# Attention and MLP on one core: seven early attention slots take the interleaved form of the later ones

## The chip, the cores and the metric

The kernel runs on one core of a Trainium2 chip. Its engines work side by side, each through its own queue in order: TensorE (PE: matmuls, with PEld for its weight loads), VectorE (DVE), ScalarE (ACT), GpSimd (POOL), and SyncE (SP), which issues DMAs. Matmuls write into banks of PSUM, an accumulator memory of eight banks here, which DVE and ACT read. An engine that has to wait for another one waits on a semaphore, and everything behind the waiting instruction in its queue waits with it. The metric is the time of one execution on the device, in microseconds (us).

## What is computed

Attention with normalised queries and keys, and after it an MLP whose activation is h - tanh(h):

```python
batch, n_heads, seq, head_dim = (8, 12, 448, 64)
q_n, k_n = (rmsnorm(q, g_q), rmsnorm(k, g_k))
scores = scale * np.matmul(q_n, k_n.transpose(0, 1, 3, 2))
attn = np.exp(scores - np.max(scores, axis=-1, keepdims=True))
attn = attn / (np.sum(attn, axis=-1, keepdims=True) + 1e-09)
attn_out = np.matmul(attn, v)
x = attn_out.transpose(0, 2, 1, 3).reshape(B * S, H * D)   # 3584 x 768
h = x @ w_in                                                # 768 x 2048
g = h - np.tanh(h)
out = g @ w_out                                             # 2048 x 768
```

All matmuls are in float32. In the profile each of them shows as two records, so "x16" in a row of PE stands for 8 matmuls.

## The kernel before

**Slots.** Attention is worked off in 48 slots, six for each of the eight batches; a slot `s` is one pair of heads of one batch. `NP` is 6, so slots 0 to 5 are the first batch, 6 to 11 the second, and so on. The MLP of batch b runs while the attention of batch b + 1 is computed. The MLP is one generator, `stream`; `run(ns)` takes matmuls from it until they are worth `ns` of PE's time. So the order of all instructions on each engine is written out by hand: a slot issues some attention work, then a stretch of the MLP ("a gap"), then attention work again. There is no scheduler after that.

**Three kinds of slot.** `first_slot` (slots -3 to 5) runs before any MLP; it also begins to round the weights (L71 and L72 on ACT, L78 to L82 on DVE, L90 on POOL, in this order for each piece). `early_slot` (6 to 11) runs beside the first batch's MLP, in which the rest of the weights is still rounded, combined (L339) and kept. `slot` (12 to 47) runs beside the others. `FOLDED` is 13: from there on a slot sums its exponentials in another way (`fold` and what follows), so that no sums are taken on PE. Four gaps make up a slot. In slots 6 to 8 a gap is 14 matmuls of 224 columns (`L791`, the first layer of the MLP, 28 records); in slots 9 to 11 it is 8 matmuls of 448 columns (`L969`, the second layer of the first batch, 16 records).

**What a slot computes.** For its two heads, with 448 keys in four chunks (three of 128, numbered 0 to 2, and a last one `KF` of 64 keys for each of the two halves of the queries):
- `scores(s + 1, c)` (L528): keys times queries of the next slot, in tiles of 64 rows and 32 columns of the array, into two banks, one for each head (`L542`); then an exponential on ACT for each bank (`L548`). Its result goes to `p` (chunks 0 and 1), `p_full` (chunk 2) and `p_last`.
- `totals(s)` (L654): the sums over the keys, as matmuls with ones (`L669`), into one bank, and a reciprocal on DVE (`L674`). Up to slot 9 there are 16 matmuls in it, later 4, because from slot 10 on DVE has added up the exponentials before (`add`, `add_last`).
- `last_values` and `values(s)` (L588, L639): values times probabilities. `values` uses tiles of 128 rows and 32 columns (`L646`): all 128 keys of a chunk at once, each bank of `av` taking one half of the queries (224 columns).
- `divide(s)` (L717): four multiplications on DVE (`L730`) take `av` times the reciprocal into `xT`, the MLP's input; for the last three pairs of heads of a batch, POOL forms sums of it (`tt`, L744 to L747).
- `turn(s + 2)` (L438): keys and queries of the slot after the next are transposed on PE (`L443`, `L447`) into two banks, and copied by ACT.

**The visit.** From slot 13 on, `visit` (L620) does values and the next slot's scores together. `half_values` (L601) takes the values in tiles of 64 rows and 32 columns (`L608`): each of the two banks of `av` gets half of the keys and all 448 queries. Four such tiles and four of the scores fit the array side by side, and `wave` issues them alternately. `divide` then adds the two banks: ACT copies one into `xT` (L722), DVE adds the other (L723), and DVE multiplies (L727).

**Banks.** Three banks (`mm`) are for the MLP. Five (`sc`) are for attention, and `sc_bank()` hands them out in turn; an engine that writes a bank waits until the reader of its former content is done. Up to slot 11 all five rotate, and `av` is two of them. Before slot 12, L1143 sets two aside as `av_banks`, so that three rotate.

**Order in an early slot.** `totals(s)`, scores of chunks 0 and 1 of the next slot, the load of v for s + 2, a gap, `turn(s + 2)` and squares, a gap, scores of chunk `KF`, `last_values`, `values`, `divide`, scores of chunk 2, and then two gaps in four halves with additions and norms between them (`add`, `add_last`, `norm`, `norm_q`; the last of these is eight scalings on ACT, `L430`, in slots 6 to 11).

Of the kernel before, what the change touches and what calls it, by code (L numbers as in the profile page):

```python
# [144 lines left out]
def bounded_path(tc, ctx, q, k, v, moe_w_in, moe_w_out, out, g_col, ident, ones, half_ones, neg_half, early):  # L145
# [379 lines left out]
    def sc_bank():  # L525
        return bank_of("sc")

    def scores(s, c, apart=False):  # L528

        rr, kT, qT = turned[s]  # L530
        n = S if c < KF else HS
        name, bufs = ("p", 2) if c < 2 else ("p_full", 1) if c < KF else ("p_last", 2)
        if c == 1:
            p = probs[s, 1] = probs[s, 0]
        else:
            p = probs[s, c] = pp.tile([P, 2, 2 if c < 2 else 1, n], F32, name=name, bufs=bufs)
        tiles = [sc_bank() for _ in range(2)]

        def score(h, i):
            at, first = (i * BL, 0) if c < KF else (i * BL % KR, i * BL // KR * n)  # L540
            r = slice(h * D, (h + 1) * D)
            nc.tensor.matmul(  # L542
                tiles[h][i * BL : (i + 1) * BL, :n], lhsT=kT[r, c * P + at : c * P + at + BL],
                rhs=qT[r, first : first + n], start=True, stop=True,
            )

        def exp(h):
            nc.scalar.activation(  # L548
                p[:, h, c if c < 2 else 0, :], tiles[h][:, :n], AF.Exp,
                scale=1.0 if rr is None else rr[:, 0, 2 * c + h : 2 * c + h + 1],  # L550
            )

        if apart:
            return [(lambda i, h=h: score(h, i), lambda h=h: exp(h)) for h in range(2)]
        for i in range(P // BL):
            for h in range(2):
                score(h, i)
        for h in range(2):
            exp(h)
# [28 lines left out]
    def last_values(s, av):  # L588

        v_nat, p = loaded["v", s], probs[s, KF]  # L590
        for n in range(2):
            keys, at = slice(n * KR, (n + 1) * KR), n * HS if s >= FOLDED else 0
            for m in range(2):
                for h in range(2):
                    r = (2 * m + h) * BL
                    nc.tensor.matmul(  # L596
                        av[n][r : r + BL, at : at + HS], lhsT=v_nat[keys, h, KF, m * BL : (m + 1) * BL],
                        rhs=p[keys, h, 0], start=(s < FOLDED), stop=False, skip_group_check=(s >= FOLDED),
                    )

    def half_values(s, c, av, first):  # L601
# [37 lines left out]
    def values(s, av, chunks=(2, 0, 1)):  # L639
        v_nat, p = loaded["v", s], full(s)  # L640
        for c in chunks:
            for n in range(2):
                for m in range(2):
                    for h in range(2):
                        r = (2 * m + h) * BL
                        nc.tensor.matmul(  # L646
                            av[n][r : r + BL, :HS], lhsT=v_nat[:, h, c, m * BL : (m + 1) * BL],
                            rhs=p[c][:, h, n * HS : (n + 1) * HS], start=False, stop=(c == 1),
                        )
        if 1 in chunks:  # L650
            del loaded["v", s]
        return av
# [21 lines left out]
        nc.vector.reciprocal(rs, dn[:, :HS])  # L674


    FOLDED = 2 * NP + 1

    def fold(s):

# [36 lines left out]
    def divide(s, av):  # L717
        b, hp = steps[s]
        rs = whole.pop(s)
        x = xT[b, hp] = xp.tile([P, S], F32, name="xT")  # L720
        if s >= FOLDED:
            nc.scalar.copy(out=x, in_=av[0][:, :S])  # L722
            nc.vector.tensor_tensor(out=x, in0=x, in1=av[1][:, :S], op=ALU.add)  # L723
        for m in range(2):
            rows = slice(m * D, (m + 1) * D)
            if s >= FOLDED:
                nc.vector.tensor_tensor(out=x[rows], in0=x[rows], in1=rs, op=ALU.mult)  # L727
                continue
            for n in range(2):
                nc.vector.tensor_tensor(  # L730
                    out=x[rows, n * HS : (n + 1) * HS], in0=av[n][rows, :HS], in1=rs[n * D : (n + 1) * D],
                    op=ALU.mult,
                )
        for c in range(NCH):
            del probs[s, c]
        if hp < HC:
            return
        c = hp - HC
        if c == 0:
            tt[b] = tp.tile([P, 3, HC, HS], F32, name="tt", bufs=1)  # L740
        eng = nc.vector if b == 0 and c == HC - 1 else nc.gpsimd
        x11, x12, x21, x22 = (xT[b, r][:, n : n + HS] for r in (c, hp) for n in (0, HS))
        t1, t2, t4 = (tt[b][:, i, c] for i in range(3))
        eng.tensor_tensor(out=t1, in0=x12, in1=x11, op=ALU.subtract)  # L744
        eng.tensor_tensor(out=t2, in0=x22, in1=t1, op=ALU.subtract)  # L745
        eng.tensor_tensor(out=x12, in0=x22, in1=x12, op=ALU.subtract)
        eng.tensor_tensor(out=t4, in0=x21, in1=t2, op=ALU.subtract)  # L747
# [264 lines left out]
    def has(s):  # L1012
        return 0 <= s < NS
# [41 lines left out]
    def early_slot(s):  # L1055
        gap = gap_ns(s)
        totals(s, sc_bank())
        if has(s + 1):
            scores(s + 1, 0)
            scores(s + 1, 1)  # L1060
        if has(s + 2):
            load(s + 2, "v")
        run(gap)
        if has(s + 2):
            turn(s + 2, sc_bank(), sc_bank())
        if has(s + 3):
            squares(s + 3)
        if has(s + 4) and not by_blocks(s + 4):
            load(s + 4, "qk")
        run(gap)  # L1070
        if has(s + 1):
            scores(s + 1, KF)
        av = [sc_bank() for _ in range(2)]
        last_values(s, av)
        divide(s, values(s, av))
        if has(s + 1):
            scores(s + 1, 2)
        for work, n in ((add, 1), (add_last, 1), (norm, 3), (norm_q, 3)):
            run(gap / 2)
            if has(s + n):  # L1080
                work(s + n)

    def slot(s):

        gap = gap_ns(s)
        av = av_banks
        if has(s + 1):
            scores(s + 1, KF)
        if s < FOLDED:
            last_values(s, av)  # L1090
            totals(s, sc_bank())
            divide(s, values(s, av))
            for c in range(KF):
                scores(s + 1, c)
        else:
            visit(s, av)
        if has(s + 2):
            load(s + 2, "v")
        rows, ahead, following = has(s + 2), has(s + 3), has(s + 1)
        folded = following and s + 1 >= FOLDED  # L1100
        first = s + 3 == TURNED

        def scale_or_turn():
            if first:
                turn(s + 2, sc_bank(), sc_bank())
            else:
                scale_blocks(s + 2)

        work = (
            ((rows, scale_or_turn),),  # L1110
            ((rows and not first, lambda: turn_blocks(s + 2, 0)), (first, lambda: load_blocks(s + 3))),
            ((rows and not first, lambda: turn_blocks(s + 2, 1)), (has(s + 4), lambda: load_blocks(s + 4))),
            ((following, lambda: add(s + 1, False)), (ahead and not first, lambda: square_blocks(s + 3))),
            ((following, lambda: add_third(s + 1)),),
            ((ahead and not first, lambda: norm_blocks(s + 3)),),
            ((following, lambda: add_last(s + 1)), (ahead and not first, lambda: meet_blocks(s + 3))),
            ((folded, lambda: fold(s + 1)),),
            ((folded, lambda: fold_rest(s + 1)), (first, lambda: square_blocks(s + 3))),
            (
                (folded, lambda: gather(s + 1, 0)), (ahead and not first, lambda: power_blocks(s + 3)),  # L1120
                (first, lambda: norm_blocks(s + 3)),
            ),
            ((folded, lambda: gather(s + 1, 1)), (first, lambda: meet_blocks(s + 3))),
            ((folded, lambda: spread_sums(s + 1)), (first, lambda: power_blocks(s + 3))),
            (),
            ((folded, lambda: turn_sums(s + 1)),),
        )
        for point in work:
            run(4 * gap / (len(work) + 1))
            for wanted, fn in point:  # L1130
                if wanted:
                    fn()
        run(4 * gap / (len(work) + 1))
# [4 lines left out]
    done[0] = 1  # L1138
    for s in range(-3, NP):
        first_slot(s)  # L1140
    for s in range(NP, 2 * NP):
        early_slot(s)
    banks["sc"], av_banks = banks["sc"][:3], banks["sc"][3:]  # L1143
    for s in range(2 * NP, NS):
        slot(s)
    run(1e9)
# [345 lines left out]
```

## Time and profile before

| | us |
|---|---|
| median of 3 runs | 1376.66 |
| lowest and highest of the 3 | 1376.35, 1377.57 |
| the profiled execution, its own time | 1375.42 |
| its span, first to last instruction | 1373.5 |

Where the slots that matter lie in the profiled execution (start of `totals` or, in slot 12, of the first scores, from the timeline of PE):

| slot | starts at | its MLP stretches |
|---|---|---|
| 6 | 75.34 | first layer, batch 0 |
| 7 | 110.58 | first layer, batch 0 |
| 8 | 145.35 | first layer, batch 0 |
| 9 | 176.07 | second layer, batch 0 |
| 10 | 208.91 | second layer, batch 0 |
| 11 | 240.85 | second layer, batch 0 |
| 12 | 272.55 | first layer, batch 1 |
| 13 | 302.89 | first layer, batch 1 |

How to read the lines of the profile. A row of a timeline has its start, its length, the engine, the line of the kernel, the operation, out<-in with the program's names, the tile of the array and the shape, and the number of records that were merged into it. In square brackets stands how long the engine stood idle before it, and what ended that. A row of waits has the waiting engine and line, what it waited for, and total, number and longest. A row of a window has the stretch, its length, and for each engine the busy time with the number of instructions, then the granted clock of PE (1.00 is full), the share of the DMA engines and GB/s. "issue" is time in which an engine waited for nothing that the profile shows.

### The profile page before, as it was taken

Reading aid. Unit: us, or ns where it says so; the run is one execution under the profiler, and the core shown is the slowest. Engines: PE = TensorE matmul, PEld = TensorE weight load, DVE = VectorE, ACT = ScalarE, POOL = GpSimd, SP = SyncE. Lnnn points to the kernel's source line nnn. Section 1 sums busy time; section 2 is a strip of 40 time slices with the busy share of each in tenths; the row PEclk is TensorE's granted clock in tenths of the full one; section 3 lists DMA queues with packets and bytes.
Section 4 is the critical chain, followed back from the end, with each engine's and each line's share of the span. In section 5 each row is a group of like instructions: output and inputs, shape, how many; then the busy total and the mean of one; then the engine's idle time right before and its main releaser. Section 6 shows DMA issues by size and latency. Waiting matters only on the chain.

```text
span 1373.5 us, 29906 instructions
## 1 busy us (share of the span) xinstructions
PE 1344.5 (98%) x11840; PEld 1126.3 (82%) x11840; DVE 888.6 (65%) x1378; ACT 551.1 (40%) x1314; POOL 555.5 (40%) x345
## 2 busy tenths in 40 slices
PE   7988999999999999999999999999999999999997
PEld 3466854479988998898899889889988998999997
DVE  5999989747855775666765578557765677533311
ACT  7855654344433444334433444334443344211100
POOL 4756665233632355315543336323463155302300
PEclk9999999999999999999999999999999999999999
DMA  7879889855675666666567657756665665556664
GB/s 167 193 201 259 252 257 248 252 147 148 208 191 135 181 186 186 150 163 197 168 164 202 163 142 203 191 146 160 196 188 155 159 196 164 143 161 183 191 190 91
DMA packets 367657, 249.91 MB, mean 182 GB/s; under 512 B 281748, under 2 KB 309780, under 8 KB 367508
## 3 DMA queue, kind: packets, MB, share of 16 engines
q1 hardware_dynamic: 367504, 247.90, 66.9%
q8 instruction: 96, 1.57, 0.5%
q14 instruction: 53, 0.43, 0.1%
q10 hardware_dynamic: 4, 0.00, 0.0%
HBM read 214.40 MB, written 33.42 MB: 180 GB/s over the span
## 4 chain that ended last, share of the span: by engine, by line
PE 93%; DMA 2%; SPq 2%; DVE 1%; ACT 1%; POOL 0%; issue 0%; ACTq 0%; POOLq 0%
PE mm L791 69%; PE sc L542 9%; PE sc L608 6%; PE mm L969 5%; PE sc L646 1%; PE sc L596 1%; DMA w_raw<-in_moe_w_in_dram 1%; PE mm L646 1%; SPq L272 1%; DMA gT<-in_moe_w_in_dram 0%; DMA w_in<-w_out 0%; PE mm L669 0%; PE sc L669 0%; SPq L125 0%; SPq L123 0%
## 5 line engine op out<-in xcount | busy, mean ns | idle before, releaser
L791 PE MATMUL mm<-xT,w_f 128*128 128x224 f32 x1392 | 275.6, 354 | 0.0
L791 PEld LDWEIGHTS mm<-xT,w_f 128*128 128x128 f32 x1392 | 262.1, 190 | 10.2 <-issue 9.5
L791 PEld LDWEIGHTS mm<-gT,w_f 128*128 128x128 f32 x1344 | 252.8, 190 | 12.8 <-issue 8.4
L791 PE MATMUL mm<-gT,w_f 128*128 128x224 f32 x1344 | 263.0, 354 | 0.0
L828 POOL TENSOR_TENSOR gT<-s,th 128x448 f32<-128x448 f32 x96 | 121.9, 1275 | 333.1 <-ACT th L827 329.4
L499 POOL TENSOR_TENSOR rr_mine<-rr_mine,neg_half 128x28 f32<-128x28 f32 x33 | 158.1, 4791 | 147.7 <-DVE rr_mine L497 96.8
L542 PE MATMUL sc<-qT,kT 64*32 64x448 f32 (+1 forms) x3072 | 213.7, 498 | 2.6 <-ACT p_last L548 1.7
L791 PE MATMUL mm<-tt,w_f 128*128 128x224 f32 x1044 | 208.6, 353 | 0.0
L791 PEld LDWEIGHTS mm<-tt,w_f 128*128 128x128 f32 x1044 | 197.1, 190 | 4.4 <-issue 4.4
L791 PE MATMUL mm<-tg,w_f 128*128 128x224 f32 x1008 | 197.5, 352 | 0.0
L791 PEld LDWEIGHTS mm<-tg,w_f 128*128 128x128 f32 x1008 | 190.7, 190 | 0.0
L542 PEld LDWEIGHTS sc<-qT,kT 64*32 64x32 f32 x3072 | 70.6, 106 | 70.4 <-issue 54.2
L723 DVE TENSOR_TENSOR xT<-xT,sc 128x448 f32<-128x448 f32 x35 | 21.7, 621 | 138.6 <-PE sc L542 94.9
L608 PE MATMUL sc<-p,v_nat 64*32 64x448 f32 x1120 | 110.5, 536 | 0.0
L745 POOL TENSOR_TENSOR tt<-xT,tt 128x224 f32<-128x224 f32 x23 | 30.3, 1317 | 168.0 <-DVE xT L727 147.3
L548 ACT ACTIVATE p<-sc 128x448 f32<-128x448 f32 x132 | 71.7, 543 | 48.2 <-PE sc L542 36.3
L827 ACT ACTIVATE th<-s 128x448 f32<-128x448 f32 x96 | 54.4, 573 | 69.3 <-DVE s L857 32.2
L698 ACT COPY sum_g<-sum 32x14 f32<-32x14 f32 x280 | 56.3, 201 | 55.1 <-DVE sum L690 43.7
L969 PE MATMUL mm<-gT,w_out 128*128 128x448 f32 x192 | 74.3, 542 | 0.0
L969 PEld LDWEIGHTS mm<-gT,w_out 128*128 128x128 f32 x192 | 35.7, 190 | 36.7 <-issue 36.4
L608 PEld LDWEIGHTS sc<-p,v_nat 64*32 64x32 f32 x1120 | 40.7, 107 | 29.9 <-issue 29.9
L142 POOL TENSOR_TENSOR rr<-rr,neg_half 112x8 f32<-112x8 f32 (+1 forms) x30 | 49.1, 1666 | 32.9 <-DVE rr L141 30.9
(151 smaller groups left out, 1819.5 us busy)
## 6 DMA issues: line engine op xcount, KB each, us to landing
w_f<-w_in SPq DMA_DIRECT2D x196, 384.0 KB, 3.6
w_f<-w_out SPq DMA_DIRECT2D x147, 512.0 KB, 4.5
w_raw<-in_moe_w_out_dram SPq DMA_DIRECT2D x16, 768.0 KB, 5.5
out_dram<-th SPq DMA_DIRECT2D x192, 56.0 KB, 3.6
w_in<-w_out SPq DMA_DIRECT2D x21, 384.0 KB, 5.3
qk_nat<-in_q_dram SPq DMA_DIRECT2D x132, 56.0 KB, 2.2
qk_nat<-in_k_dram SPq DMA_DIRECT2D x132, 56.0 KB, 2.3
v_nat<-in_v_dram SPq DMA_DIRECT2D x72, 96.0 KB, 4.1
```

Of the source, the lines that this page charges most:

```text
L142: nc.gpsimd.tensor_tensor(out=r, in0=r, in1=neg_half[:rows], op=ALU.pow)
L499: nc.gpsimd.tensor_tensor(out=mine, in0=mine, in1=neg_half[:, :1].to_broadcast([P, 2 * NJ]), op=ALU.pow)
L542: nc.tensor.matmul(tiles[h][i * BL : (i + 1) * BL, :n], lhsT=kT[r, c * P + at : c * P + at + BL], rhs=qT[r, first : first + n], start=True ...
L548: nc.scalar.activation(p[:, h, c if c < 2 else 0, :], tiles[h][:, :n], AF.Exp, scale=1.0 if rr is None else rr[:, 0, 2 * c + h : 2 * c + h ...
L608: nc.tensor.matmul(av[g][i * BL : (i + 1) * BL, :S], lhsT=v_nat[keys, h, c, m * BL : (m + 1) * BL], rhs=p[keys, h], start=first, stop=True ...
L646: nc.tensor.matmul(av[n][r : r + BL, :HS], lhsT=v_nat[:, h, c, m * BL : (m + 1) * BL], rhs=p[c][:, h, n * HS : (n + 1) * HS], start=False, ...
L698: nc.scalar.copy(out=acc[h * BL : (h + 1) * BL, g], in_=part[g * BL : (g + 1) * BL, h * NJ : (h + 1) * NJ])
L745: eng.tensor_tensor(out=t2, in0=x22, in1=t1, op=ALU.subtract)
L791: nc.tensor.matmul(bank[:, f * HS : (f + 1) * HS], lhsT=w[:, c * width + f, :], rhs=moving[p](c), start=(first and f == 0 and c == 0), sto ...
L827: nc.scalar.activation(th, h, AF.Tanh, bias=0.0, scale=1.0)
L828: eng.tensor_tensor(out=g[:, rows, cols], in0=h, in1=th, op=ALU.subtract)
L969: nc.tensor.matmul(bank[:, :S], lhsT=w_out_row(f, n // HC)[:, n % HC * P : (n % HC + 1) * P], rhs=g[:, f, :], start=(f == 0), stop=(f == C ...
```

## The change

Slots 6 to 12 take the visit that slots 13 to 47 already have. For that:
- `last_values` and `divide` use the form of the visit from slot 6 (`HALVED`) on instead of slot 13 (`FOLDED`). The reciprocal of slots 6 to 12 still has its own layout, one row block for each half of the queries, so that `divide` has four multiplications in these slots, now out of `xT`.
- An early slot issues `totals(s)`, the next slot's scores of chunk `KF`, the visit with `divide` and the scores of chunk 2, the load of v, and then its gaps, with `turn` between the first and the second. In slot 12 the sums come first as well.
- The three rotating banks and the two of `av` are split off before slot 6 instead of before slot 12.

```diff
-            keys, at = slice(n * KR, (n + 1) * KR), n * HS if s >= FOLDED else 0
+            keys, at = slice(n * KR, (n + 1) * KR), n * HS if s >= HALVED else 0
...
-    FOLDED = 2 * NP + 1
+    HALVED, FOLDED = NP, 2 * NP + 1
...
-        if s >= FOLDED:
+        if s >= HALVED:
             nc.scalar.copy(out=x, in_=av[0][:, :S])
             nc.vector.tensor_tensor(out=x, in0=x, in1=av[1][:, :S], op=ALU.add)
...
             for n in range(2):
+                part_of = x[rows, n * HS : (n + 1) * HS]
                 nc.vector.tensor_tensor(
-                    out=x[rows, n * HS : (n + 1) * HS], in0=av[n][rows, :HS], in1=rs[n * D : (n + 1) * D],
-                    op=ALU.mult,
+                    out=part_of, in0=part_of if s >= HALVED else av[n][rows, :HS],
+                    in1=rs[n * D : (n + 1) * D], op=ALU.mult,
                 )
...
         totals(s, sc_bank())
         if has(s + 1):
-            scores(s + 1, 0)
-            scores(s + 1, 1)
+            scores(s + 1, KF)
+        visit(s, av_banks)
         if has(s + 2):
             load(s + 2, "v")
         run(gap)
...
         run(gap)
-        if has(s + 1):
-            scores(s + 1, KF)
-        av = [sc_bank() for _ in range(2)]
-        last_values(s, av)
-        divide(s, values(s, av))
-        if has(s + 1):
-            scores(s + 1, 2)
         for work, n in ((add, 1), (add_last, 1), (norm, 3), (norm_q, 3)):
...
         gap = gap_ns(s)
-        av = av_banks
+        if s < FOLDED:
+            totals(s, sc_bank())
         if has(s + 1):
             scores(s + 1, KF)
-        if s < FOLDED:
-            last_values(s, av)
-            totals(s, sc_bank())
-            divide(s, values(s, av))
-            for c in range(KF):
-                scores(s + 1, c)
-        else:
-            visit(s, av)
+        visit(s, av_banks)
...
+    banks["sc"], av_banks = banks["sc"][:3], banks["sc"][3:]
     for s in range(NP, 2 * NP):
         early_slot(s)
-    banks["sc"], av_banks = banks["sc"][:3], banks["sc"][3:]
     for s in range(2 * NP, NS):
         slot(s)
```

More of the change, by code (lines that the diff above doesn't have):

```diff
@@ L597, in last_values @@
                         av[n][r : r + BL, at : at + HS], lhsT=v_nat[keys, h, KF, m * BL : (m + 1) * BL],
-                        rhs=p[keys, h, 0], start=(s < FOLDED), stop=False, skip_group_check=(s >= FOLDED),
+                        rhs=p[keys, h, 0], start=(s < HALVED), stop=False, skip_group_check=(s >= HALVED),
                     )
```

## The prediction

> **What bounds the kernel now.** I read the busy shares first, then the waits of PE between 80 and 282 us (the slots that the change touches, 6 to 12), then the timelines of PE and DVE there. All times are of the profiled execution, whose span is 1373.5 us.
>
> ```profile
> PE 1344.5 (98%) x11840; PEld 1126.3 (82%) x11840; DVE 888.6 (65%) x1378; ACT 551.1 (40%) x1314; POOL 555.5 (40%) x345
> ```
> PE sets the time, and what it loses anywhere stays lost. By stage:
> ```profile
> 76.00:110.00 34.00, 29.44 (x270) 24.32 (x263) 33.24 (x47) 17.77 (x30) 16.57 (x9) 1.00 0.76 212
> 110.00:145.00 35.00, 30.90 (x283) 25.59 (x282) 33.31 (x42) 21.41 (x40) 22.64 (x13) 1.00 0.90 263
> 145.00:176.00 31.00, 31.00 (x283) 25.48 (x281) 29.97 (x42) 17.81 (x35) 20.57 (x12) 1.00 0.81 250
> ```
> The columns are stretch, length, then busy time of PE, weight loads, DVE, ACT, POOL, and the granted clock. In slots 6 to 8 DVE is busy 96.5 of 100 us: it rounds the weights while the first MLP runs. Here both engines bind. How far DVE lags behind PE shows in its reciprocals, one for each slot:
> ```profile
> 76.48 0.56 PE L669 MATMUL sc<-p_last,half_ones 128*32 128x224 f32 x8
> ...
> 85.40 0.65 PE L443 MATMUL sc<-ident,k_nat 128*128 128x128 f32 x4 [1.20 <-DVE rs L674]
> ...
> 111.74 0.56 PE L669 MATMUL sc<-p_last,half_ones 128*32 128x224 f32 x8
> ...
> 123.83 0.66 PE L443 MATMUL sc<-ident,k_nat 128*128 128x128 f32 x4 [2.61 <-DMA w_in<-w_out]
> ```
> ```profile
> 83.79 1.56 DVE L674 RECIPROCAL rs<-sc 128x224 f32<-128x224 f32 x1
> ...
> 122.22 1.55 DVE L674 RECIPROCAL rs<-sc 128x224 f32<-128x224 f32 x1
> ...
> 152.56 1.55 DVE L674 RECIPROCAL rs<-sc 128x224 f32<-128x224 f32 x1
> ...
> 180.91 1.54 DVE L674 RECIPROCAL rs<-sc 128x224 f32<-128x224 f32 x1
> ...
> 213.59 1.56 DVE L674 RECIPROCAL rs<-sc 128x224 f32<-128x224 f32 x1
> ...
> 244.40 1.56 DVE L674 RECIPROCAL rs<-sc 128x224 f32<-128x224 f32 x1
> ```
> The sums of slot 6 leave PE at 76.97 (the next row's start), and the reciprocal that reads their bank ends at 85.35: 8.4 us. For slots 7 to 11 the same lag is 11.5, 7.1, 4.7, 5.7 and 4.6 us (sums out at 112.23, 147.00, 177.72, 209.49, 241.36). Today nothing needs that bank until the turn (L443), a gap of 28 records later, since five banks rotate. Even so L443 waits 1.20 us for it in slot 6 and 2.61 in slot 7 (put down to a DMA, but the reciprocal ended at 123.77, 0.06 before).
>
> **The change, part by part.**
>
> *Matmul work.* Values of a slot stay 24 matmuls, now in half-height tiles of 448 columns instead of full-height ones of 224. The slot that already runs this way shows the price:
> ```profile
> 303.29 0.96 PE L608 MATMUL sc<-p_full,v_nat 64*32 64x448 f32 x16
> 304.04 0.54 PE L542 MATMUL sc<-qT,kT 64*32 64x448 f32 x1
> ...
> 307.05 0.58 PE L596 MATMUL sc<-p_last,v_nat 64*32 64x224 f32 x16
> ```
> From first to last it takes 302.89 to 308.32, 5.4 us. An early slot now spends 2.1 on sums and scores (209.49 less 0.6 to 211.16) and 4.3 (224.22 to 228.62), 6.4; after, 5.4 + 0.5 = 5.9. Saved: 0.5 a slot, 3.0 over slots 6 to 11. Slot 12 takes 272.55 to 280.67, 8.1, against 5.9: saved 2.2, and its wait of 0.3 with it.
>
> *Vector and scalar work.* ACT copies one half (0.52, L722), DVE adds the other (0.62, or 0.53 in a run of them, L723); four multiplications stay four of about 0.4 us. The copy lies in ACT's free half; the add is on DVE's path in slots 6 to 8.
>
> *Moved with it.* A slot's exponentials come in one run on ACT instead of two; 6 to 8 us of ACT's weight steps that stood between them come after, where DVE reaches them later still: nothing. The load of v (three DMAs of SP, L117 and L125) is issued behind the visit; it lands 4.1 us after issue and is read two slots later, over 60 us: nothing, 4.1 at most without that cover. SP passes no weight load with it, since these are issued inside the MLP's stretches.
>
> *The new wait.* The rotation has three banks now: sums take one, the last score chunk two, and the first scores inside the visit come back to the sums' bank. So PE stops there until the reciprocal has read it. Between lie only the last chunk's scores (0.40, 94.49 to 94.90) and the first values (0.75, 303.29 to 304.04): cover 1.15 us against lags of 4.6 to 11.5. Everything behind it on PE waits too, the MLP first of all. Then the wait turns round: in DVE's order the add and multiplications now follow the reciprocal directly, and they need values that PE could not start. From that point of slot 13 (304.04) to its DVE add (308.45) are 4.4 us; with 0.06 for the release DVE stands idle 4.5, and the weights queued behind stand with it. No other work covers either hole, both queues being in order.
>
> *Slots 6 to 8.* DVE is the bound, so a slot costs its hole and the add: 4.5 + 0.5 = 5.0. PE's lost 7.2 us (8.4 - 1.15) of slot 6 do not add up with that: PE later skips the waits of 2.54 and 1.20 or meets them as late as DVE. In slot 7 I followed the rows: the MLP of that gap starts after the visit, and DVE, at L853, waits about 1.6 more for a product that used to be done. 3 x 5.0 + 1.6 = 16.6.
>
> *Slots 9 to 11.* PE has no wait here, so a slot costs its stall less 0.5. Slot 9: 4.7 - 1.15 - 0.5 = 3.1. In slot 10 DVE is about 1.1 further behind (it lost 5.0 in slot 9 and had idle time of 2.1 and 1.9 there to make up): 5.7 + 1.1 - 1.15 - 0.5 = 5.1. Slot 11: 4.6 - 1.15 - 0.5 = 3.0, up to 1.5 more if DVE doesn't catch up in an idle time of 1.53 before it; I take 3.5.
>
> *Slot 12.* The reciprocal still ends at 275.76, behind a transposition at 273.22; PE would come to the bank at about 274.1: 1.7 lost, 2.5 saved, -0.8.
>
> Sum: 16.6 + 3.1 + 5.1 + 3.5 - 0.8 = 27.5.
>
> *PE after a stall.* Two places of the trace price it:
> ```profile
> 10.07 3.24 PE L542 MATMUL sc<-qT,kT 64*32 64x448 f32 x32 [0.62 <-ACT qT L451]
> ...
> 27.85 1.73 PE L542 MATMUL sc<-qT,kT 64*32 64x448 f32 x32
> ...
> 39.15 0.96 PE L669 MATMUL mm<-p,ones 128*32 128x224 f32 x16
> ...
> 67.88 1.72 PE L669 MATMUL mm<-p,ones 128*32 128x224 f32 x16 [0.46 <-DVE xT L730]
> ```
> After idle stretches PE runs at half speed for about 3.2 us (10.07 to 13.24; 67.88 to 71.03), though the granted clock reads 1.00: 1.6 us lost. After 2.61 us (123.83) it does not. Bounds for one stall: 0 (that row) to 1.6. My stalls of 6 to 10 us lie beyond both; I take 1.6 for slots 6, 7, 8, 10 and half of it for 9 and 11, whose 3.5 us lie between: 8.0. It lengthens the visit, and so DVE's hole too. Against it, DVE's rounding steps run 0.55 to 2.1 us for one shape, long where POOL works at the same time, and a hole lets POOL run alone: 0 to 1 a slot in slots 6 to 8; I take 0.5, -1.5 in all.
>
> The Trainium skill, "TensorE: Matmul & The Clock Gate", Part 1, says the array falls to half clock after an idle window of about 3.4 us and needs as long to come back. Row 67.88 disagrees in part: one wait of 1.98 and one of 0.46, with only two rows of transpositions between, sufficed; Part 4 says that transpositions don't count as busy. By the page's figures the term would be estimated at 1.7 each for five stalls, 8.5 instead of 8.0.
>
> 27.5 + 8.0 - 1.5 = +34.0 us, a span of 1407.5. The profiled run's own time is 1375.42 and the median 1376.66; on the median the forecast is 1410.7.
>
> **The rivals.**
> - *The stall without the half clock.* The mechanism above, PE at full speed after it, as after the 2.61 us at 123.83: 27.5 - 1.5, 1402.7. For it: the granted clock is 1.00 in every stage. Against: 10.07 and 67.88. 20%.
> - *The backlog drains once.* While PE stands in slot 6, DVE works off its lag; if the later reciprocals are then on time, slot 6 costs 6.6, the others perhaps 1 each: +12, 1389. For it: DVE's idle time in slot 9. Against: DVE loses as much as PE in the same slot, and 30 of 31 us of slot 8 are work. 14%.
> - *ACT is late too.* Scores' exponentials queue behind the scaling of q (eight of L430, 2.0 us, waiting on POOL's power). In slot 9 they would end at 184.65, after the reciprocal's 182.45. If this is so in four slots, 2 us each: 1419. Against: in slots 7, 8, 10 and 11 they end 0 to 1.5 us before it. 8%.
> - *The faster side.* The reciprocal is there when PE comes, because the lag is under 1.15 us in every slot; then only 3.0 and 2.5 are saved: 1371. It decides where the lag crosses 1.15, and no slot of seven shows that. 6%.
>
> **How the numbers follow.** 52% for the forecast, 1410.7 with 6 either way (the unknown half clock in slots 9 and 11, POOL's relief, the 1.5 of slot 11). The range must take in the first rival below and the ACT one above: 1396 to 1421. A measurement of this kernel can't tell less than about 0.2% (2.8 us) from nothing. Faster by more: 0.06; within: 0.02 (the drained backlog at its best); slower: 0.92.
>
> **What would show it.** PE idle before L542 in slots 6 to 11, released by DVE's L674, about 7, 10, 7, 4, 6 and 4 us; DVE idle before L723 of 4 to 6 us in the same slots; waves of scores at half speed behind the longest stalls; all from slot 13 on as before, only later. No PE wait on L674 would make it wrong; stalls that shrink after slot 6 would speak for the drained backlog.

## The result and the profile after

| | before | after |
|---|---|---|
| median, us | 1376.35 (1375.29 to 1377.57, 5 runs) | 1418.52 (1417.6 to 1419.84, 5 runs) |
| span of the profiled execution, us | 1373.5 | 1416.2 |
| mean granted clock | 0.997 | 0.981 |

The changed kernel takes 1.0306 times as long (95% interval 1.0292 to 1.032): 42 us slower, where 34 were forecast. The busy shares and the clock row of the page of after (2.5% of the span for each digit):

```profile
PE 1350.8 (95%) x11840; PEld 1125.9 (80%) x11840; DVE 896.4 (63%) x1385; ACT 557.4 (39%) x1321; POOL 553.8 (39%) x345
...
PEclk9988999999999999999999999999999999999999
```

PE has the same number of records as before and only 6.3 us more busy time, but its share falls from 98 to 95%: it stands idle. Who makes it wait shows in the waits of after between 76 and 320 us (total, number, longest):

```profile
PEld sc L542 <- DVE rs L674: 46.7, 7, 11.1
...
PE sc L542 <- DVE rs L674: 41.1, 7, 10.3
DVE xT L723 <- PE sc L542: 39.9, 6, 7.3
```

The first scores of the visit (L542) wait for the reciprocal (L674), and DVE's addition (L723) waits nearly as long for PE. In the same stretch of the kernel before, L542 waits 0.3 us in all, for ACT. The timeline of PE in after has one such stall in each of the slots 6 to 12:

```profile
85.52 0.95 PE L542 MATMUL sc<-qT,kT 64*32 64x448 f32 x1 [8.64 <-DVE rs L674]
...
130.91 0.95 PE L542 MATMUL sc<-qT,kT 64*32 64x448 f32 x1 [10.28 <-DVE rs L674]
...
170.58 0.95 PE L542 MATMUL sc<-qT,kT 64*32 64x448 f32 x1 [6.78 <-DVE rs L674]
...
207.04 0.95 PE L542 MATMUL sc<-qT,kT 64*32 64x448 f32 x1 [4.67 <-DVE rs L674]
...
245.47 0.95 PE L542 MATMUL sc<-qT,kT 64*32 64x448 f32 x1 [4.20 <-DVE rs L674]
...
284.40 0.95 PE L542 MATMUL sc<-qT,kT 64*32 64x448 f32 x1 [5.30 <-DVE rs L674]
...
318.61 0.56 PE L542 MATMUL sc<-qT,kT 64*32 64x448 f32 x1 [1.26 <-DVE rs L674]
```

The second column says more than the stall: behind the first six the same matmul takes 0.95 us, behind the last 0.56. And DVE's side of slot 6, from the timeline of DVE in after:

```profile
81.74 0.55 DVE L78 TENSOR_SCALAR w_out<-w_out 128x768 f32<-128x768 f32 x1
82.32 0.56 DVE L79 TENSOR_SCALAR w_out<-w_out 128x768 int32<-128x768 int32 x1
82.92 0.96 DVE L82 SCALAR_TENSOR_TENSOR w_out<-gT,w_out 128x768 int32<-128x768 int32 x1
83.91 1.56 DVE L674 RECIPROCAL rs<-sc 128x224 f32<-128x224 f32 x1
92.11 0.62 DVE L723 TENSOR_TENSOR xT<-xT,sc 128x448 f32<-128x448 f32 x1 [6.64 <-PE sc L542]
```

The reciprocal comes behind a weight piece, as late as before the change (83.79 there). PE waits for its end, 85.47, and then DVE stands for 6.64 us until PE has done the visit. The later holes are 6.13, 6.78, 7.32, 6.88 and 6.19 us, 4.49 in slot 12; the forecast had 4.5 before the half clock.

Starts of the sums of each slot, from both timelines of PE, give the loss by slot (for slot 12, where its scores of the last chunk or its sums start; the end of it is the start of slot 13):

| slot | lasts before | lasts after | longer by | forecast |
|---|---|---|---|---|
| 6 | 35.24 | 43.73 | 8.49 | 6.1 |
| 7 | 34.77 | 43.16 | 8.39 | 7.7 |
| 8 | 30.72 | 38.59 | 7.87 | 6.1 |
| 9 | 32.84 | 39.87 | 7.03 | 3.9 |
| 10 | 31.94 | 37.98 | 6.04 | 6.7 |
| 11 | 31.70 | 38.25 | 6.55 | 4.3 |
| 12 | 30.34 | 29.66 | -0.68 | -0.8 |

Up to the start of slot 6 the profiled execution of after is 1.45 us ahead, because it has no half-clocked stretch like the one at 67.88 of before. The code there is the same, so I take this for an accident of the executions profiled. Together 42.24, of a difference of the spans of 42.7: the loss lies in the slots that were changed. (The forecast's column holds its half clock, 1.6 or 0.8, and POOL's -0.5 in slots 6 to 8.)

How much of it is the half clock? From the first wave to the next row of the MLP, a visit of after takes 6.43 us in slot 6 (85.52 to 91.95), then 5.93, 6.56, 7.11, 6.66 and 5.98. In slot 13 of before, at full speed, it is 4.28 (304.04 to 308.32). Over the six slots 13.0 us more. The granted clock shows it, if the window is as narrow as the visit. Two windows of after, of slots 6 and 12 (columns as in the windows shown before, the clock third from the end):

```profile
85.40:92.40 7.00, 6.88 (x98) 2.54 (x99) 0.36 (x2) 3.17 (x6) 0.43 (x1) 0.68 1.02 304
...
316.00:323.00 7.00, 5.74 (x133) 2.36 (x129) 2.41 (x2) 5.65 (x16) 0.00 (x0) 1.00 0.82 187
```

0.68 against 1.00. In the page's 40 slices, 35 us each, the same is an 8 or a 9.

### The profile page after: what moved, and what is told of

It reads as the page before. It is cut to its first block, busy times and chain, and to the rows that moved or that the text cites. A ratio compares the mean times of both kernels' runs of the same rounds, so it can differ in the third digit from the quotient of the medians.

```text
span 1416.2 us, 29909 instructions
## 1 busy us (share of the span) xinstructions
PE 1350.8 (95%) x11840; PEld 1125.9 (80%) x11840; DVE 896.4 (63%) x1385; ACT 557.4 (39%) x1321; POOL 553.8 (39%) x345
## 4 chain that ended last, share of the span: by engine, by line
PE 86%; DVE 7%; DMA 2%; SPq 2%; ACT 1%; issue 1%; POOL 0%; ACTq 0%; DVEq 0%; POOLq 0%
PE mm L792 64%; PE sc L542 9%; PE sc L608 7%; PE mm L970 3%; PE sc L596 1%; DVE w_out L78 1%; DMA w_raw<-in_moe_w_in_dram 1%; DVE w_out L79 1%; DVE w_out L82 1%; PE mm L646 1%; DVE rs L674 1%; SPq L272 1%; PE mm L669 0%; SPq L125 0%; DMA w_raw<-in_moe_w_out_dram 0%
## 5 line engine op out<-in xcount | busy, mean ns | idle before, releaser
L542 PE MATMUL sc<-qT,kT 64*32 64x448 f32 (+1 forms) x3072 | 234.4, 516 | 43.0 <-DVE rs L674 41.1
L542 PEld LDWEIGHTS sc<-qT,kT 64*32 64x32 f32 x3072 | 77.4, 109 | 111.9 <-issue 54.2
L608 PE MATMUL sc<-p,v_nat 64*32 64x448 f32 x1344 | 146.0, 579 | 0.0
L723 DVE TENSOR_TENSOR xT<-xT,sc 128x448 f32<-128x448 f32 x42 | 26.1, 621 | 182.9 <-PE sc L542 139.3
L548 ACT ACTIVATE p<-sc 128x448 f32<-128x448 f32 x132 | 71.9, 545 | 48.0 <-PE sc L542 36.2
L608 PEld LDWEIGHTS sc<-p,v_nat 64*32 64x32 f32 x1344 | 50.5, 114 | 42.4 <-issue 42.4
L970 PEld LDWEIGHTS mm<-gT,w_out 128*128 128x128 f32 x192 | 36.0, 190 | 35.6 <-issue 35.5
```

Of the source, the lines that this page charges most:

```text
L542: nc.tensor.matmul(tiles[h][i * BL : (i + 1) * BL, :n], lhsT=kT[r, c * P + at : c * P + at + BL], rhs=qT[r, first : first + n], start=True ...
L548: nc.scalar.activation(p[:, h, c if c < 2 else 0, :], tiles[h][:, :n], AF.Exp, scale=1.0 if rr is None else rr[:, 0, 2 * c + h : 2 * c + h ...
L608: nc.tensor.matmul(av[g][i * BL : (i + 1) * BL, :S], lhsT=v_nat[keys, h, c, m * BL : (m + 1) * BL], rhs=p[keys, h], start=first, stop=True ...
L970: nc.tensor.matmul(bank[:, :S], lhsT=w_out_row(f, n // HC)[:, n % HC * P : (n % HC + 1) * P], rhs=g[:, f, :], start=(f == 0), stop=(f == C ...
```

## The experiments

Ratios stand to the kernel before, with their 95% intervals; "us over before" is the difference of the two medians of the same comparison. The diffs are against the changed kernel, but for the second, which is against the kernel before, and the seventh, which is against the first experiment's.

**The wait taken away by distance.** The last chunk's scores and the visit go behind the two first gaps, as the old form had them; sums stay in front.

```diff
         totals(s, sc_bank())
-        if has(s + 1):
-            scores(s + 1, KF)
-        visit(s, av_banks)
         if has(s + 2):
             load(s + 2, "v")
         run(gap)
...
         run(gap)
+        if has(s + 1):
+            scores(s + 1, KF)
+        visit(s, av_banks)
```

> The changed kernel with one thing moved: in slots 6 to 11 the two first gaps of the MLP stand between the sums and the visit again. If the loss is the wait for the reciprocal, the cover grows from 1.15 us to over 12, more than the longest lag of 11.5, PE has no wait on L674 in slots 6 to 11, and only the saving of the visit is left: 1374 (1371 to 1377). If the visit itself or the three banks cost (the rival), it stays at 1385 or more.

Measured: 1382.95 (1381.98 to 1384.52), ratio 1.0053 [1.0039, 1.0067]: between the theory and its rival. 35.6 of the 42 us came back, not all. PE's stalls on L674 in slots 6 to 11 are gone; one of 1.3 us in slot 12 is left. Slots 9 and 11 now last 0.47 us less than before the change and slot 12 0.69 less: that is the visit's own saving, forecast as 0.5 and 0.8 (in slot 12 net of that wait). What is still lost lies in slots 6, 7 and 8 (2.35, 1.25 and 1.41 us) and in slot 10 (5.98). For slot 10, two rows of ACT and three of PE of this kernel:

```profile
230.92 0.89 ACT L71 ACTIVATE w_out<-w_raw 128x768 f32<-128x768 f32 x1 [3.48 <-DMA w_raw<-in_moe_w_out_dram]
...
232.91 0.78 ACT L548 ACTIVATE p_last<-sc,rr 128x224 f32<-128x224 f32 x2
```
```profile
214.83 0.57 PE L669 MATMUL sc<-rows,ones 128*32 128x224 f32 x4 [1.30 <-DVE rows L586]
...
233.41 0.56 PE L542 MATMUL sc<-qT,kT 64*32 64x448 f32 x1 [2.20 <-ACT p_last L548]
...
234.47 0.95 PE L608 MATMUL sc<-p,v_nat 64*32 64x448 f32 x1
```

ACT waits for a weight load, the exponentials of the last chunk stand behind it, and the visit, which needs a bank back from them, waits 2.20 us and then falls to half speed. The sums of slot 10 wait too, 1.30 us, for DVE's last addition of exponentials (L586). The kernel before has no such wait but no margin either: there L586 ends at 208.93, and the sums begin at 208.91. In slot 7 of the same kernel DVE, the bound there, waits for the visit, which now ends later than the old values did:

```profile
134.10 0.62 DVE L862 TENSOR_TENSOR s<-mm,s 128x448 f32<-128x448 f32 x1
137.79 0.62 DVE L723 TENSOR_TENSOR xT<-xT,sc 128x448 f32<-128x448 f32 x1 [3.08 <-PE sc L542]
```

So the wait carries most of the loss, and the visit in these slots isn't free even without it.

**Only the banks.** The kernel before, with its old order and old tiles; the three rotating banks and the two of `av` are split before slot 6.

```diff
-        av = [sc_bank() for _ in range(2)]
+        av = av_banks
...
+    banks["sc"], av_banks = banks["sc"][:3], banks["sc"][3:]
     for s in range(NP, 2 * NP):
         early_slot(s)
-    banks["sc"], av_banks = banks["sc"][:3], banks["sc"][3:]
```

> The kernel before with one thing of the change: the three rotating banks and the two fixed ones are split off before slot 6. No visit, no new order. If the wait for the sums' bank is the loss, it is here too: the scores of chunk 1 come back to that bank 0.8 us after the sums in slots 6 to 11, PE waits on L674 for about 7, 10, 6, 4, 5 and 4 us, and the time is 1400 to 1412. If the visit's tiles or its place are the loss (rival), 1377.

Measured: 1409.01 (1407.74 to 1410.01), ratio 1.0237 [1.0221, 1.0252]; 32.7 us over before, as expected. The timeline of PE in this kernel:

```profile
85.52 1.75 PE L542 MATMUL sc<-qT,kT 64*32 64x448 f32 x16 [8.16 <-DVE rs L674]
...
126.22 1.75 PE L542 MATMUL sc<-qT,kT 64*32 64x448 f32 x16 [8.23 <-DVE rs L674]
...
163.59 1.75 PE L542 MATMUL sc<-qT,kT 64*32 64x448 f32 x16 [4.77 <-DVE rs L674]
```

With neither a visit nor a new order, scores of chunk 1 come back to the sums' bank behind those of chunk 0, and wait as the visit does; 16 records in 1.75 us are again half speed (0.98 at full speed). Three banks in rotation are enough to lose most of it. The Trainium skill, "Perfetto Trace Analysis", section "Optimization Strategy", says that the same gap repeated on the engine that should be saturated can mean too little PSUM for the next tile; this run shows such a case, six gaps of 1.88 to 8.23 us, 31.1 in all.

**The reciprocal's bank held out.** The sums' bank is left out of the rotation until the visit has been issued, so that two rotate.

```diff
+    held = []
+
     def sc_bank():
-        return bank_of("sc")
+        bank = bank_of("sc")
+        while any(bank is b for b in held):
+            bank = bank_of("sc")
+        return bank
...
-        totals(s, sc_bank())
+        held.append(sc_bank())
+        totals(s, held[0])
...
         visit(s, av_banks)
+        held.pop()
```

> The changed kernel, but the bank of the sums is left out of the rotation until the visit is over, so that scores in the visit use two banks and wait for exponentials alone. The theory: the wait on L674 is gone, but behind it stands one on L548, because the exponentials of the last chunk queue behind the scaling of q (L430) in slots 7 to 11, by 8, 5, 5, 3 and 2 us from the rows of before; slot 6 is free: 1398 (1390 to 1405). If the reciprocal is the only late thing (rival): 1373.

Measured: 1409.72 (1409.08 to 1411.86), ratio 1.0252 [1.0236, 1.0267]. The direction was right, the size not: only 9 us came back, and the time lies above the range. The waits of this kernel between 76 and 320 us (its lines are 5 higher: L547 is L542, L553 is L548, L679 is L674), and the row of ACT ahead of the longest:

```profile
PE sc L547 <- ACT p_last L553: 27.3, 5, 8.8
...
PE sc L547 <- DVE rs L679: 1.2, 1, 1.2
```
```profile
120.07 2.02 ACT L430 ACTIVATE n<-q_nat,rr 112x64 f32<-112x64 f32 x8 [5.49 <-POOL rr L142]
121.99 0.76 ACT L553 ACTIVATE p_last<-sc,rr 128x224 f32<-128x224 f32 x2
```

With the wait on DVE away, the same instruction waits for ACT, whose exponentials stand behind the scaling of q, which waits 5.49 us for POOL. It is the mechanism of the rival "ACT is late too", hidden as long as DVE came later.

**All three banks for scores.** The sums of slots 6 to 11 go to one of the MLP's banks. They can overwrite products that the MLP still holds there, so a part of the output is wrong; only the time of this kernel is of use.

```diff
-        totals(s, sc_bank())
+        totals(s, bank_of("mm"))
```

> The sums of slots 6 to 11 go into one of the MLP's three banks, so that all three rotating banks are left to scores (with the sums' bank merely held out, two were left). Theory (three engines in a ring; behind the sums' bank stands the next late reader, ACT's exponentials of the last chunk): the first scores of the visit no longer wait on the reciprocal, but one of their two banks comes back from the last chunk, so PE still waits on p_last's exponentials, some 20 to 30 us in slots 7 to 11 as with the bank held out: 1403 to 1412. Rival (the wait on the exponentials came from having two banks only): it falls under 10 us, and the time to 1385 to 1392. In both, the MLP's own wait on the reciprocal, two banks later, stays under 3 us a slot.

Measured: 1402.12 (1401.01 to 1403.49), ratio 1.0187 [1.017, 1.0204]: neither theory. The waits of PE in this kernel between 76 and 320 us:

```profile
PE sc L542 <- ACT p_last L548: 15.9, 4, 7.3
PE mm L669 <- DVE gT L829: 6.2, 1, 6.2
PE mm L669 <- DVE rs L674: 4.3, 1, 4.3
```

The wait on the exponentials falls from 27.3 to 15.9 us, and the sums themselves wait 10.5 us for a bank of the MLP's that DVE has still to read. Of the 11.4 us less, 6.2 are those of slot 8, where the sums now wait 6.2 us first, so that they only moved. In slots 7, 9, 10 and 11 the wait is 1.1 to 1.5 us shorter; that may be the third bank, and no run shows it by itself. In the arrangements tried here, what one holder of a bank gains another waits for.

**Matmuls in front of the wait.** 8, 10, 6, 4, 4 and 3 full matmuls that nothing reads are put where PE stands idle in slots 6 to 11.

```diff
+        for i in range((8, 10, 6, 4, 4, 3)[s - NP]):
+            nc.tensor.matmul(
+                av_banks[i % 2][:, :S], lhsT=ident, rhs=turned[s + 1][1], start=True, stop=True
+            )
         visit(s, av_banks)
```

> The changed kernel with matmuls whose results nothing reads in front of the wait in slots 6 to 11 (8, 10, 6, 4, 4 and 3 of 0.77 us, each series shorter than the wait), so that PE is not idle long. They leave the output as it is. If the half clock behind a stall is real time, the visits run at full speed and 10 us come back: 1408 (1405 to 1412), the waits for L674 shorter by the series. If it is not (rival), 1418.

Measured: 1411.1 (1409.89 to 1412.94), ratio 1.0259 [1.0243, 1.0275]: 7.4 us less than the changed kernel by the medians, 6.5 by the ratios, with the same data waits and more work. The rows of PE of this kernel in slots 6, 7, 8 and 11:

```profile
85.87 0.56 PE L542 MATMUL sc<-qT,kT 64*32 64x448 f32 x1 [0.63 <-DVE rs L674]
...
129.15 0.56 PE L542 MATMUL sc<-qT,kT 64*32 64x448 f32 x1 [2.43 <-DVE rs L674]
...
168.89 0.56 PE L542 MATMUL sc<-qT,kT 64*32 64x448 f32 x1 [1.90 <-DVE rs L674]
...
276.86 0.68 PE L542 MATMUL sc<-qT,kT 64*32 64x448 f32 x1 [3.03 <-DVE rs L674]
```

The visits that follow take 4.30, 6.00, 4.30 and 5.99 us (to the next rows of the MLP at 90.17, 135.15, 173.19 and 282.85); slots 9 and 10 have 5.55, with a second wait in it, and 4.30. In this kernel the half clock is gone where the idle time was cut to 1.90 or less, and not where 2.43 and 3.03 were left. The visits of slots 6, 8, 9 and 10 are shorter than in the changed kernel by 2.13, 2.26, 1.56 and 2.36, together 8.3, against the 6.5 to 7.4 us that the time fell. So most of the half clock is time on the path.

**DVE's hole filled.** `divide` (copy, addition, four multiplications) is issued behind the second gap, so that DVE has weights and products queued behind the reciprocal.

```diff
-        divide(s, av)
+        if not NP <= s < 2 * NP:
+            divide(s, av)
...
         run(gap)
+        divide(s, av_banks)
         for work, n in ((add, 1), (add_last, 1), (norm, 3), (norm_q, 3)):
```

> The changed kernel, but in slots 6 to 11 the copy, the addition and the multiplications of divide are issued behind the second gap, so that DVE goes on with the weights after the reciprocal. If DVE's idle time behind the reciprocal is half of the mechanism, DVE keeps its pace, its lag runs out after slot 7, and 1382 is left (1379 to 1390): about 6.5 in slot 6, 1 to 2 in slot 7, nothing after. If only PE's own waits count (rival), the six waits stay and the time is 1410 to 1418.

Measured: 1422.2 (1421.89 to 1425.3), ratio 1.0345 [1.0329, 1.0361]. Nothing came back, the time lies above the rival's range too, and the theory falls. DVE and ACT in slot 6 of this kernel (L675 is L674):

```profile
83.61 1.56 DVE L675 RECIPROCAL rs<-sc 128x224 f32<-128x224 f32 x1
...
86.58 0.96 DVE L82 SCALAR_TENSOR_TENSOR w_out<-gT,w_out 128x768 int32<-128x768 int32 x1
93.14 0.56 DVE L78 TENSOR_SCALAR w_out<-w_out 128x768 f32<-128x768 f32 x1 [5.59 <-ACT w_out L71]
```
```profile
87.05 0.63 ACT L548 ACTIVATE p<-sc,rr 128x448 f32<-128x448 f32 x1 [8.72 <-PE sc L542]
...
92.20 0.90 ACT L71 ACTIVATE w_out<-gT 128x768 f32<-128x768 f32 x1
```

DVE goes on with one weight piece and then stands all the same. The next piece comes from ACT, which stands behind exponentials that wait for PE, which waited for DVE. PE still waits 32.4 us on the reciprocal here. In this slot three in-order queues form a ring, so that moving the addition alone does not fill DVE's hole.

**The last chunk one gap earlier.** The kernel of the first experiment, with `scores(s + 1, KF)` ahead of the second gap, so that slot 10's wait on the exponentials goes.

```diff
+        if has(s + 1):
+            scores(s + 1, KF)
         run(gap)
-        if has(s + 1):
-            scores(s + 1, KF)
         visit(s, av_banks)
```

> The first experiment (two gaps between sums and visit) with the last chunk's scores issued one gap before the visit. In that experiment slot 10 took 37.9 us instead of 31.9, as its exponentials stood in ACT's queue behind a weight step that waited for a DMA, while the visit came to their bank. If that was it, slot 10 falls to 31.5, PE's waits on L548 in slots 6 to 11 are gone, and the time is 1377 (1375 to 1380). If slot 10's loss has another cause, it stays at 1383.

Measured: 1387.33 (1386.43 to 1387.69), ratio 1.0078 [1.0064, 1.0092]: slower than without it. The wait on `p_last` in slot 10 is gone, yet slot 10 lasts 34.79 us and not 31.5: the sums' wait of 1.30 us on L586 is still there. And slot 8 lasts 36.47 us instead of 32.13. The row of PE in this kernel:

```profile
161.35 0.61 PE L542 MATMUL sc<-qT,kT 64*32 64x224 f32 x14 [3.16 <-ACT kT L445]
```

Scores that come right behind `turn` wait for ACT's copy of the keys just turned.

**Only slot 12.** Slots 6 to 11 as before; slot 12 has the sums in front and the visit.

```diff
-    HALVED, FOLDED = NP, 2 * NP + 1
+    HALVED, FOLDED = 2 * NP, 2 * NP + 1
```

(`early_slot` and the place of the split are those of the kernel before.)

> The change for slot 12 alone; slots 6 to 11 as before. In the changed kernel slot 12 was 0.7 us shorter than before, with a wait of 1.3 on L674. So 1375 (1374 to 1376), no difference that can be told. If the visit costs by itself in a slot with sums on PE (rival): 1378 or more.

Measured: 1375.83 (1374.88 to 1377.31, 11 runs), ratio 0.9996 [0.9987, 1.0005]. As expected, a saving of 0.7 us can't be told from nothing.

**Slots 9 to 11 in the new form.** Slots 6 to 8 as before. Slots 9 to 11 have the order of the seventh experiment (the last chunk one gap earlier), and slot 12's sums and slot 13's last chunk inside slot 11.

```diff
+    for s in range(NP, HALVED):
+        early_slot(s)
     banks["sc"], av_banks = banks["sc"][:3], banks["sc"][3:]
-    for s in range(NP, 2 * NP):
-        early_slot(s)
+    for s in range(HALVED, 2 * NP):
+        late_early_slot(s)
```

(`HALVED` is 9 here; `early_slot` is that of the kernel before.)

> Meant to beat both: slots 6 to 8 as before, where DVE has no time to spare; slots 9 to 11 with the visit behind two gaps and the last chunk's scores one gap ahead; the sums of slot 12 and the last chunk's scores for slot 13 three quarters through slot 11. No wait on L674 is left from slot 9 on: 0.5 saved in each of slots 9 to 11 and 2.5 in slot 12, 1372 (1370 to 1375). If lateness of ACT or DVE shows again behind it: 1376 or more.

Measured: 1381.28 (1379.8 to 1382.0), ratio 1.0034 [1.0021, 1.0046]: 4.9 us slower than before instead of faster. Slot 9, where most of it is lost (36.6 us instead of 32.84), in the rows of PE of this kernel:

```profile
178.27 6.28 PE L970 MATMUL mm<-gT,w_out 128*128 128x448 f32 x16
...
187.50 0.61 PE L542 MATMUL sc<-qT,kT 64*32 64x224 f32 x14 [1.63 <-ACT kT L445]
188.03 7.98 PE L970 MATMUL mm<-gT,w_out 128*128 128x448 f32 x16
```

A wait of 1.63 us right behind the transpositions costs itself and 1.70 in the next MLP stretch, which runs partly at half speed. Slot 10 lasts 34.80 us instead of 31.94, again with the sums' wait of 1.30 us on L586. No version that was tried is measurably faster than the kernel before; the visit's own saving, 0.5 a slot, is about what six slots together would just make visible.

## Why the prediction came out as it did

The direction and the mechanism were right, the size was off by 8 us. The sum, step by step:

- **The new wait.** Right: PE waits on the sums' bank in every changed slot, for 8.64, 10.28, 6.78, 4.67, 4.20, 5.30 and 1.26 us; forecast about 7, 10, 7, 4, 6 and 4, and 1.7 in slot 12. That the rotation of three is what does it was shown by the split alone (32.7 us over before, where the whole change has 42), and the distance put between sums and visit took the waits of slots 6 to 11 away.
- **PE after a stall.** This is the term that was mis-sized: 8.0 forecast, 13.0 measured, in all six slots and 1.65 to 2.83 us each. I gave half of 1.6 to stalls of some 3.5 us, by the row at 123.83; these were 4.67 and 5.30, and lost 2.83 and 1.70. And my sentence that the granted clock reads 1.00 there was wrong in one of the two places. For 10.00 to 13.30 it does (why the rows there take twice their time all the same stays open), but a narrow window of before shows 0.50 at the other place:

```profile
67.80:71.10 3.30, 3.22 (x40) 1.46 (x47) 3.17 (x6) 1.24 (x3) 2.70 (x3) 0.50 1.04 230
```

- **POOL's relief.** 1.5 us forecast for slots 6 to 8. Without the half clock (2.15, 1.65 and 2.28) these slots lost 6.34, 6.74 and 5.59, together 18.7, where 16.6 were forecast ahead of that relief and 15.1 with it: 3.6 too little. No run took the relief by itself, so whether there is any is not shown.
- **Slots 6 to 8, hole and addition.** The holes were sized well: 6.64, 6.13 and 6.78 us, less the half clock of the same visits, are 4.5 each. But the reasoning that DVE has its hole because the additions stand behind the reciprocal was incomplete: with `divide` moved away DVE stood 5.59 us in slot 6, now for ACT. The row that I followed in slot 7 was there (L854 waits 1.53 us for a product).
- **Slots 9 to 11.** Without the half clock 4.20, 3.66 and 4.85, together 12.7, against 11.7. The single slots were off by 1.1 to 1.4 both ways, so that the near sum is partly luck.
- **Matmul work and slot 12.** The visit saves 0.47 where nothing waits, forecast 0.5. (The times quoted for it, of slot 10, give 2.25 and 4.40, together 6.65, and so 0.7; the 0.5 fits slot 11, where 2.18 and 4.24 make 6.42.) Slot 12 gains 0.68, forecast 0.8, and that is luck in part: its 2.5 counted the wait of 0.3 twice, as the 8.1 hold it already. From its start to the MLP the slot takes 7.44 us after, 1.26 of them the wait, against 8.12: 1.94 saved and 1.26 lost, not 2.5 and 1.7.
- The rest of the difference is the 1.45 us ahead of slot 6, which I take for an accident: 5.0 + 3.6 + 1.0 + 0.1 - 1.45 = 8.2.

Of the rivals, **the stall without the half clock** falls by the clock and by the matmuls put in front of the wait. **The backlog drains once** falls: the stalls of slots 7 to 11 don't vanish after slot 6; in slot 7 the reciprocal again ends 11.6 us after the sums (11.5 before the change). **ACT is late too** was not what happened, but it is what stands next, as the experiments with the bank held out and with the MLP's bank show. **The faster side** falls with the first stall.

Open: how the 5.0 us that slots 6 to 8 still lose without the wait divide between the addition (0.5 to 0.6 each by its rows), DVE's hole of 3.08 and other things; what makes up the 9.5 us between the split alone and the whole change; and whether a version with the visit behind the gaps in slots 9 and 11 alone would show its 0.5 each, which was not tried and would lie under what can be measured.

## What to carry to other kernels

Count the banks in rotation against the lag of the engine that frees them: take the time from the last write of a bank to the end of its reader, in the slots in question, and compare it with the work that lies between two uses. A form that costs nothing where the reading engines have slack can cost the whole of their lag where they are loaded, and the lost time is not theirs to make up if they wait for the stalled engine too. Before taking one late reader out of the way, look who comes next in the same bank, since the next one may be nearly as late.

## What the runs showed of the hardware

Waits far shorter than the stalls I reckoned with halve PE's speed for a time. After 2.20 us (the first experiment) and 2.43 us (the matmuls in front of the wait) the first rows still run at 0.56 and the rows from about 1.1 and 1.8 us later at 0.95; after 4.2 us and more the first row already takes 0.95. After 1.26 and 1.90 us nothing is lost, yet 1.88 in the run with the banks alone halved the very next row (274.60, 16 records in 1.75 us), 1.63 behind transpositions cost 1.70, and 2.61 ahead of transpositions, at 123.83 of before, cost nothing. Nearly the same two waits, 1.98 and 0.46 us ahead of 67.88 in before, 1.92 and 0.46 ahead of 67.98 in after, halved the rows behind them in before and not in after. So the length of a wait alone doesn't decide it in these runs. The Trainium skill, "TensorE: Matmul & The Clock Gate", Part 1, puts both the idle window and the recovery at about 3.4 us; the recovery fits as a lower bound (twice what the six visits of after lost, as an estimate of their time at half speed, is 3.3 to 5.7 us), the waits of 2.20 and 2.43 do not.
